# Dense layer with SiLU on one core: where the tail's wait stands, which queue loads the first weight slab, how many dummies, and how the last weight columns are cut

## The chip, the core and the metric

The kernel runs on one core of a Trainium2 chip. The metric is the device time of one execution in microseconds (us). The kernel before took 126.45 us in the median of three runs (126.36 to 126.84). One more execution was profiled; its own time was 126.87 us, and its span, from the first to the last instruction, is 125.4 us.

TensorE (PE) multiplies, ScalarE (ACT) applies the activation, VectorE (DVE) copies results out of PSUM, and SyncE (SP) mostly issues DMAs. ACT can issue DMAs too.

## The reference

```python
# x [1, 2048, 640], w1 [640, 1728], w2 [1728, 640], all bf16
h = einsum("bsd,df->bsf", x, w1)
h = silu(h)
out = einsum("bsf,fd->bsd", h, w2)
```

## The kernel before

**Layout.** The inner width is 1728 = 13 x 128 + 64. Thirteen tiles of 128 rows (`FT`) and a tail of 64 rows (`FL`) make up the hidden layer, kept transposed in `hT` (tokens along the free side) and, for the tail, in `hTt`. The 2048 tokens are cut into four chunks of 512 (`SCH`). The depth 640 of the first product is five tiles of 128 (`DT`).

**The opening.** x must be turned; a transposing DMA writes it to `xT`. A few instructions are moved by `early()` (line 97) ahead of the barrier with which every program begins: the turned load of x for chunk 0, depth tiles 0 and 1 (line 121, on SP); the first half (tiles 0 to 3) of the first weight slab (line 122, on ACT); a memset of `z`; and 20 dummy matmuls on `z` (128x256 each, lines 127 to 135), which keep PE at work until the first data is there. After the barrier SP issues in this order: the second half of the first slab (`ld_w1b`, line 139), slab 1, x tiles 2 and 3, slabs 2 and 3, x tile 4, slab 4, then in one load the columns 1024 to 1727 of all five depth tiles (`ld_rest`, line 146, 880 KB), then 15 turned loads for chunks 1 to 3 of x (line 154), and last w2. ACT, past its barrier, loads its activation table and runs a small activation (line 148).

**First product, chunk 0.** Lines 183 to 193 go depth first: for each of the five depth tiles, PE sweeps the first eight tiles of 128 columns (`NO` = 8) into eight PSUM banks, so that each sweep needs one slab only. Forty matmuls of 128x512 come out of this. Within the first sweep PE waits for `ld_w1b` at tile 4. After the last sweep tiles 8 to 12 follow (lines 203 to 209), five matmuls each, behind one wait for `ld_rest`. ACT turns each finished bank into `hT` (`silu`, line 168).

**First product, the rest.** Chunks 1 to 3 (lines 210 to 217) run tile by tile, each chunk behind a wait for its five turned loads. Then the tail (lines 219 to 227): for each pair of chunks ten matmuls of half the columns, two at a time in two halves of the array, and one ACT activation into `hTt`. `h_last` is the last activation of the full tiles, `h_tail` holds the two of the tail.

**Second product.** `quad()` (line 327) works on four outputs at a time. Each output is a sum over thirteen tiles, which are taken as halves of 64 rows so that two outputs run side by side in the two halves of the array (`lanes`, line 311), plus one matmul on the tail. The order within one half of the work is fixed by `begin()`:

```python
return [lambda ft=ft: u.half(r0, ft, ft == 0, False) for ft in range(FT)] + [end]
```

So thirteen halves come first for each of the two outputs, 26 matmuls in all, and the matmul on the tail (`u.tail()`, in `end`) is the fourteenth. Before the first `quad` stands the wait at line 342 for `h_last` and for both of `h_tail`. The first `quad` does the last 128 of the 640 output columns for all tokens (`Wide`), turned back by DMAs; the others do 512 columns for 128 tokens each (`Tok`). PSUM banks are handed out in turn by `bank()`; each waits for whatever emptied it last. `wait()` (line 69) leaves out a wait for a semaphore value that the same engine has already waited for.

Of the kernel before, what the change touches and what calls it, by code (L numbers as in the profile page):

```python
# [9 lines left out]
def bass_standalone__dense_activation_silu__prompt_kernel(  # L10
# [12 lines left out]
    F = w1.shape[1]  # L23
    P = 128
# [13 lines left out]
    pe, act, dve, pool, sp = nc.tensor, nc.scalar, nc.vector, nc.gpsimd, nc.sync  # L38

    with ExitStack() as es:  # L40
        def sb(name, shape, dtype):
            return es.enter_context(nc.sbuf_tensor(name, shape, dtype))

        xT = sb("xT", [P, DT, S], bf16)
        w1s = sb("w1s", [P, DT, F], bf16)
# [13 lines left out]
        def sem(name):  # L59
            s = es.enter_context(nc.semaphore(name))  # L60
            count[s.name if hasattr(s, "name") else name] = 0
            return [s, 0]

        def tick(ins, s, n=1):
            ins.then_inc(s[0], n)
            s[1] += n
            return (s, s[1])

        def wait(eng, *points):
            for pt in points:  # L70
                if pt is None:
                    continue
                s, v = pt
                key = (id(eng), id(s))
                if seen.get(key, 0) < v:
                    eng.wait_ge(s[0], v)
                    seen[key] = v
# [6 lines left out]
        def load(eng, out_ap, in_ap):  # L84
            s = sem(f"s_ld{n_dma[0]}")
            n_dma[0] += 1
            return tick(eng.dma_start(out=out_ap, in_=in_ap), s, 16)  # L87

        def turned(c0, c1, k0, k1):
            s = sem(f"s_tr{n_dma[0]}")  # L90
            n_dma[0] += 1
            return tick(sp.dma_start_transpose(  # L92
                out=xT[:, k0:k1, c0:c1], in_=xf[c0:c1, k0 * P:k1 * P]), s, 16)

        ET = mybir.EngineType

        def early(emit, engine, arrived=True):
            n = len(nc.main_func.blocks[0].instructions)
            r = emit()
            lst = nc.main_func.blocks[0].instructions  # L100
            new = lst[n:]
            del lst[n:]
            at = next(
                i for i, ins in enumerate(lst)
                if ins.opcode == ("EventSemaphore" if arrived else "Drain") and ins.engine == engine
            )
            lst[at:at] = new
            return r

        w1_v = w1.rearrange("(dt p) f -> p dt f", p=P)  # L110
        w2_v = w2[0:F0, :].rearrange("(ft p) d -> p ft d", p=P)

        NO = NB
        CO = NO * P

        def slab(eng, k, f0=0, f1=NO):
            return load(eng, w1s[:, k, f0 * P:f1 * P], w1_v[:, k, f0 * P:f1 * P])
# [2 lines left out]
        ld_t = {}  # L120
        ld_t[0] = ld_t[1] = early(lambda: turned(0, SCH, 0, 2), ET.SP)
        ld_w1[0] = early(lambda: slab(act, 0, 0, 4), ET.Activation)
        p_z = early(lambda: tick(dve.memset(z[:, :], 0.0), s_dve), ET.DVE, False)  # L123

        bank_free = [None] * NB

        def dummies(n):
            for _ in range(n):
                pe.matmul(ps[:, 3, 0:HB], lhsT=z[:, 0:P], rhs=z[:, :], start=True, stop=True)  # L129

        def first_dummies():
            wait(pe, p_z)
            dummies(20)

        early(first_dummies, ET.PE)

        p_warm = tick(pool.memset(warm[:, :], 0.0), s_pool)  # L137

        ld_w1b = slab(sp, 0, 4, NO)
        ld_w1[1] = slab(sp, 1)  # L140
        ld_t[2] = ld_t[3] = turned(0, SCH, 2, 4)
        ld_w1[2] = slab(sp, 2)
        ld_w1[3] = slab(sp, 3)
        ld_t[4] = turned(0, SCH, 4, 5)
        ld_w1[4] = slab(sp, 4)
        ld_rest = load(sp, w1s[:, :, CO:F], w1_v[:, :, CO:F])
        wait(act, p_warm)
        act.activation(out=warm[:, :], in_=warm[:, :], func=ACT.Silu)  # L148

# [15 lines left out]
        def mm(o, l, r, start, stop, shared=False):  # L165
            return pe.matmul(o, lhsT=l, rhs=r, start=start, stop=stop, skip_group_check=shared)  # L166

        def silu(out_ap, in_ap, bank, after):
            wait(act, after)
            r = tick(act.activation(out=out_ap, in_=in_ap, func=ACT.Silu), s_act)  # L170
            bank_free[bank] = r
            return r
# [24 lines left out]
        def bank():  # L197
            b = nxt[0] % NB
            nxt[0] += 1
            wait(pe, bank_free[b])  # L200
            return b

        wait(pe, ld_rest)
        for ft in range(NO, FT):
            b = bank()
            for k in range(DT):
                ins = mm(ps[:, b, :], w1s[:, k, ft * P:(ft + 1) * P], xT[:, k, 0:SCH],
                         start=(k == 0), stop=(k == DT - 1))
            silu(hT[:, ft, 0:SCH], ps[:, b, :], b, tick(ins, s_pe))
        for c in range(1, NSC):  # L210
            wait(pe, ld_xc[c])
            for ft in range(FT):
# [4 lines left out]
                h_last = silu(hT[:, ft, c * SCH:(c + 1) * SCH], ps[:, b, :], b, tick(ins, s_pe))  # L217
        h_tail = []
# [97 lines left out]

        def begin(u, r0):
            def end():
                u.halfway = tick(u.tail(), s_pe)
            return [lambda ft=ft: u.half(r0, ft, ft == 0, False) for ft in range(FT)] + [end]  # L320

# [5 lines left out]
        def quad(A, B, C, E):  # L327
            A.open()
            B.open()
            lanes(begin(A, 0), begin(B, HP))  # L330
            C.open()
            E.open()
            lanes(begin(C, 0), begin(E, HP))
            for X, Y in ((A, B), (C, E)):
                dx, dy = [], []
                wait(pe, X.halfway, Y.halfway)
                lanes(rest(Y, 0, dy), rest(X, HP, dx))
                X.close(dx[0])
                Y.close(dy[0])

        wait(pe, *ld_w2)
        wait(pe, h_last, *h_tail)
        quad(Wide(0), Wide(1), Wide(2), Wide(3))
        last = None
        for q in range(NSC // 2):
# [56 lines left out]
```

## Time and profile before

| what | value |
|---|---|
| median of three runs | 126.45 us |
| profiled execution, its own time | 126.87 us |
| its span | 125.4 us |
| PE busy | 121.7 us (97%) |
| ACT busy | 38.9 us (31%) |
| DVE busy | 6.9 us (6%) |
| DMA, mean rate over the span | 83 GB/s |

The profile can be asked for groups of instructions, for waits, for the chain of work that ended last, for the work in order of time, for DMAs with their time from issue to landing, and for busy time in chosen stretches. Times in such rows are counted from the start of the span. A matmul's row gives its start and an end that is modelled; matmuls overlap, so the distance between two starts tells the pace. "SPq" and "ACTq" are those engines' issuing of DMAs.

### The profile page before, as it was taken

Reading aid. Unit: us, or ns where it says so; the run is one execution under the profiler, and the core shown is the slowest. Engines: PE = TensorE matmul, PEld = TensorE weight load, DVE = VectorE, ACT = ScalarE, POOL = GpSimd, SP = SyncE. Lnnn points to the kernel's source line nnn. Section 1 sums busy time; section 2 is a strip of 40 time slices with the busy share of each in tenths; the row PEclk is TensorE's granted clock in tenths of the full one; section 3 lists DMA queues with packets and bytes.
Section 4 is the critical chain, followed back from the end, with each engine's and each line's share of the span. In section 5 each row is a group of like instructions: output and inputs, shape, how many; then the busy total and the mean of one; then the engine's idle time right before and its main releaser. Section 6 shows DMA issues by size and latency. Waiting matters only on the chain.

```text
span 125.4 us, 1834 instructions
## 1 busy us (share of the span) xinstructions
PE 121.7 (97%) x822; PEld 60.3 (48%) x828; DVE 6.9 (6%) x11; ACT 38.9 (31%) x67; POOL 0.3 (0%) x5
## 2 busy tenths in 40 slices
PE   8999999999999999999979999999999999999993
PEld 6544344444444444444435555555555555555452
DVE  0000000000000000000000022002200310220201
ACT  4000985555555555555530011001100200110110
POOL 1000000000000000000000000000000000000000
DMA  6999756546990000000000003401300220022032
GB/s 134 234 257 305 163 114 73 100 92 104 363 336 4 0 5 0 3 0 0 0 0 5 0 0 84 89 0 73 136 0 5 105 105 0 5 105 105 0 118 91
DMA packets 18823, 10.38 MB, mean 83 GB/s; under 512 B 13440, under 2 KB 18304, under 8 KB 18816
## 3 DMA queue, kind: packets, MB, share of 16 engines
q1 hardware_dynamic: 18528, 10.08, 31.6%
q10 hardware_dynamic: 288, 0.20, 0.6%
q8 instruction: 6, 0.10, 0.4%
q14 instruction: 1, 0.01, 0.0%
HBM read 4.51 MB, written 2.62 MB: 57 GB/s over the span
## 4 chain that ended last, share of the span: by engine, by line
PE 86%; DMA 6%; SPq 4%; issue 1%; ACT 1%
PE ps L166 86%; DMA w1s<-in_w_dram 6%; SPq L87 2%; SPq L92 2%; ACT hTt L170 0%; ACT o_sb L238 0%
## 5 line engine op out<-in xcount | busy, mean ns | idle before, releaser
L166 PE MATMUL ps<-xT,w1s 128*128 128x512 bf16 (+1 forms) x275 | 58.9, 381 | 0.4 <-DMA w1s<-in_w_dram 0.2
L166 PE MATMUL ps<-w2s,hT 64*128 64x512 bf16 (+3 forms) x402 | 46.3, 370 | 0.2 <-issue 0.2
L166 PEld LDWEIGHTS ps<-xT,w1s 128*128 128x128 bf16 (+1 forms) x280 | 26.5, 99 | 32.6 <-DMA w1s<-in_w_dram 0.7
L170 ACT ACTIVATE hT<-ps 128x512 bf16<-128x512 f32 x52 | 30.1, 605 | 30.0 <-PE ps L166 29.9
L166 PEld LDWEIGHTS ps<-w2s,hT 64*128 64x128 bf16 (+1 forms) x403 | 23.8, 95 | 21.4 <-issue 0.4
L238 ACT CAST o_sb<-ps 128x512 bf16<-128x512 f32 (+1 forms) x9 | 4.9, 550 | 41.6 <-PE ps L166 41.6
L166 PE MATMUL ps<-hT,w2s 64*128 64x512 bf16 x104 | 11.8, 377 | 0.8 <-ACT hTt L170 0.8
L166 PEld LDWEIGHTS ps<-hT,w2s 64*128 64x128 bf16 x104 | 5.8, 94 | 6.4 <-issue 1.2
L236 DVE CAST o_sb<-ps 128x512 bf16<-128x512 f32 (+1 forms) x8 | 5.4, 675 | 40.6 <-PE ps L166 40.6
L236 DVE CAST oT<-ps 128x512 bf16<-128x512 f32 x2 | 1.4, 692 | 75.6 <-PE ps L166 75.6
L129 PE MATMUL ps<-z 128*128 128x256 bf16 x20 | 4.5, 420 | 0.4 <-DVE z L123 0.4
L238 ACT CAST oT<-ps 128x512 bf16<-128x512 f32 x2 | 1.2, 586 | 11.4 <-PE ps L166 11.4
L129 PEld LDWEIGHTS ps<-z 128*128 128x128 bf16 x20 | 2.9, 148 | 1.5 <-DVE z L123 0.4
L166 PE MATMUL ps<-w2t,hTt 64*128 64x512 bf16 (+2 forms) x17 | 3.0, 364 | 0.0
L170 ACT ACTIVATE hTt<-ps 128x512 bf16<-128x512 f32 x2 | 1.2, 597 | 1.1 <-PE ps L166 1.1
L148 ACT ACT_TABLE_LOAD x1 | 1.3, 1283 | 0.7 <-DVEq L387 0.7
L166 PEld LDWEIGHTS ps<-w2t,hTt 64*128 64x128 bf16 x17 | 1.0, 94 | 0.9
L166 PE MATMUL ps<-hTt,w2t 64*128 64x512 bf16 x4 | 0.8, 376 | 0.0
L166 PEld LDWEIGHTS ps<-hTt,w2t 64*128 64x128 bf16 x4 | 0.2, 94 | 0.2
L148 ACT ACTIVATE warm<-warm 128x32 f32<-128x32 f32 x1 | 0.2, 230 | 0.0
L123 DVE MEMSET z<- 128x128 uint32 x1 | 0.2, 165 | 0.2 <-issue 0.2
L137 POOL MEMSET warm<- 128x32 f32 x1 | 0.1, 124 | 0.3 <-POOLq L387 0.3
(4 smaller groups left out, 0.4 us busy)
## 6 DMA issues: line engine op xcount, KB each, us to landing
out_dram<-o_sb SPq DMA_DIRECT2D x15, 160.0 KB, 1.8
w2s<-in_w_dram SPq DMA_DIRECT2D x1, 1120.0 KB, 6.4
w1s<-in_w_dram SPq DMA_DIRECT2D x4, 256.0 KB, 4.1
w2s<-in_w_dram SPq DMA_DIRECT2D x1, 960.0 KB, 8.6
w1s<-in_w_dram SPq DMA_DIRECT2D x1, 880.0 KB, 7.2
xT<-in_x_dram SPq DMA_TRANSPOSE x18, 3.8
w2t<-in_w_dram SPq DMA_DIRECT2D x2, 80.0 KB, 8.0
w1s<-in_w_dram ACTq DMA_DIRECT2D x1, 128.0 KB, 2.4
```

The lines of the kernel that those rows point to most:

```text
L87: return tick(eng.dma_start(out=out_ap, in_=in_ap), s, 16)
L92: return tick(sp.dma_start_transpose(out=xT[:, k0:k1, c0:c1], in_=xf[c0:c1, k0 * P:k1 * P]), s, 16)
L123: p_z = early(lambda: tick(dve.memset(z[:, :], 0.0), s_dve), ET.DVE, False)
L129: pe.matmul(ps[:, 3, 0:HB], lhsT=z[:, 0:P], rhs=z[:, :], start=True, stop=True)
L137: p_warm = tick(pool.memset(warm[:, :], 0.0), s_pool)
L148: act.activation(out=warm[:, :], in_=warm[:, :], func=ACT.Silu)
L166: return pe.matmul(o, lhsT=l, rhs=r, start=start, stop=stop, skip_group_check=shared)
L170: r = tick(act.activation(out=out_ap, in_=in_ap, func=ACT.Silu), s_act)
L236: r = tick(dve.tensor_copy(out=out_ap, in_=in_ap), s_dve)
L238: r = tick(act.copy(out=out_ap, in_=in_ap), s_act)
```

## The change

Four edits. The second half of the first w1 slab is issued by ACT, ahead of the barrier and right behind the first half, and no longer by SP behind it. The dummies go from 20 to 15. The last load of w1 is cut in two, columns 1024 to 1279 (tiles 8 and 9) and columns 1280 to 1727 (tiles 10 to 12 and the tail), and PE waits for the second only at tile 10. The wait for the tail activations leaves the head of the second product; it stands in `end`, right before the matmul that reads `hTt`.

```diff
@@ -120,6 +120,7 @@
         ld_w1[0] = early(lambda: slab(act, 0, 0, 4), ET.Activation)
+        ld_w1b = early(lambda: slab(act, 0, 4, NO), ET.Activation)
         p_z = early(lambda: tick(dve.memset(z[:, :], 0.0), s_dve), ET.DVE, False)
@@ -130,20 +131,21 @@
         def first_dummies():
             wait(pe, p_z)
-            dummies(20)
+            dummies(15)
...
-        ld_w1b = slab(sp, 0, 4, NO)
         ld_w1[1] = slab(sp, 1)
...
-        ld_rest = load(sp, w1s[:, :, CO:F], w1_v[:, :, CO:F])
+        CM = CO + 2 * P
+        ld_rest = load(sp, w1s[:, :, CO:CM], w1_v[:, :, CO:CM])
+        ld_rest2 = load(sp, w1s[:, :, CM:F], w1_v[:, :, CM:F])
@@ -203,6 +205,8 @@
         wait(pe, ld_rest)
         for ft in range(NO, FT):
             b = bank()
+            if ft == NO + 2:
+                wait(pe, ld_rest2)
@@ -316,6 +320,7 @@
             def end():
+                wait(pe, *h_tail)
                 u.halfway = tick(u.tail(), s_pe)
@@ -339,7 +344,7 @@
         wait(pe, *ld_w2)
-        wait(pe, h_last, *h_tail)
+        wait(pe, h_last)
         quad(Wide(0), Wide(1), Wide(2), Wide(3))
```

## The prediction

> **What bounds the kernel now.** I began with the page's busy times: PE is busy for 121.7 of 125.4 us, so anything that shortens the kernel must let PE begin useful work sooner, run it at full pace, or remove a hole. The chain of waits, in order of time, shows the holes:
>
> ```profile
> 6.72 0.04 issue
> 6.77 7.24 DMA w1s<-in_w_dram
> 14.01 0.05 issue
> 14.05 8.59 PE ps L166 x39
> ...
> 64.01 0.02 issue
> 64.03 0.61 ACT hTt L170
> 64.64 0.14 issue
> 64.77 52.96 PE ps L166 x488
> ```
>
> There are two. Up to 14.01 the chain is not PE's but the landing of the 880 KB load (issued at 6.77); at 64.03 PE stands until the second tail activation is done. From 64.77 to 117.7 it is PE alone, so what is gained by then is kept to the end. Next the work of PE in order of time, in the opening and in four very narrow stretches around 4.6, 5.5, 5.7 and 5.9 us, where a row's start is that of the matmul that was running:
>
> ```profile
> 0.39 4.45 PE L129 MATMUL ps<-z 128*128 128x256 bf16 x20 [0.39 <-DVE z L123]
> 4.63 0.63 PE L166 MATMUL ps<-xT,w1s 128*128 128x512 bf16 x1
> 5.06 0.82 PE L166 MATMUL ps<-xT,w1s 128*128 128x512 bf16 x2
> 5.49 0.61 PE L166 MATMUL ps<-xT,w1s 128*128 128x512 bf16 x2
> 5.72 0.59 PE L166 MATMUL ps<-xT,w1s 128*128 128x512 bf16 x2
> ```
>
> The starts tell the pace. Useful matmuls begin at 4.63, are 0.43 us apart up to 5.49, and 0.216 us from then on. The dummies, half as wide, stand (4.63 - 0.39)/20 = 0.212 us apart. So PE runs at half pace for the first 5.1 us of its work, although the granted clock reads 1.00 in every stretch. Third, the DMAs by issue, for the first turned load of x (issued at 0.08), the ACT load and `ld_w1b` (issued at 1.55):
>
> ```profile
> xT<-in_x_dram SPq DMA_TRANSPOSE x1, 3.5
> w1s<-in_w_dram ACTq DMA_DIRECT2D x1, 128.0 KB, 2.4
> w1s<-in_w_dram SPq DMA_DIRECT2D x1, 128.0 KB, 3.1
> ```
>
> What the first useful matmul needs is there at 0.08 + 3.5 = 3.58 us (x) and 0.21 + 2.4 = 2.6 us (weights). PE reaches it at 4.63, because 20 dummies stand ahead of it. Last, the stretches, of which I use the DMA share (second number from the right) and GB/s:
>
> ```profile
> 1.00:2.00 1.00, 1.00 (x7) 0.74 (x5) 0.00 (x0) 1.00 (x1) 0.00 (x0) 1.00 0.63 143
> 2.00:3.00 1.00, 1.00 (x7) 0.69 (x6) 0.00 (x0) 0.25 (x2) 0.00 (x0) 1.00 1.22 259
> 3.00:4.00 1.00, 1.00 (x7) 0.69 (x6) 0.00 (x0) 0.00 (x0) 0.00 (x0) 1.00 0.80 139
> ```
>
> The DMA engines are full from 2 to 3 us, while the turned load is moving, and not before.
>
> **Edit 1: 15 dummies, and `ld_w1b` on ACT.** Five dummies fewer are 5 x 0.212 = 1.06 us: the last one gives way at 3.57, just when x lands now. But `ld_w1b` is issued right behind its first half, at about 0.21 + 0.38 = 0.6 us, so its 131 KB move beside the turned load. At the 259 GB/s of that second they are 0.51 us of DMA time. If they fit into the free share of 1 to 2 us, x lands at 3.58 as now; if all of it is pushed ahead of x, at 4.09. I take 3.9, nearer the full end because most of the turned load moves in the full second. PE starts at most 0.1 later (0.04 from landing to matmul at 14.01, and a weight load of 0.15 in part beside it): 4.0, bounds 3.6 to 4.2. That is 0.63 us earlier, and leaves PE idle from 3.57 to 4.0.
>
> Not all of it counts. If full pace comes at 5.49 again, the half-paced steps cost: before, two steps, 2 x (0.427 - 0.216) = 0.42 us; after, (5.49 - 4.0)/0.427 = 3.5 steps, 0.74. Net gain 0.63 - 0.32 = **0.31 us**. Bounds: full pace by 4.0 gives 0.63 + 0.42 = 1.05; the late clock is a rival below. The Trainium skill, page "TensorE: Matmul & The Clock Gate", Part 1, says that the clock gate opens after a free-running window of about 3.4 us of busy work, whatever the kernel's start. By that rule 5.49 is a draw which another execution would not repeat, the front would be worth anything from nothing to 1.05, and a hole among the dummies could cost a window. The page "DMA: Bandwidth & Descriptors", section "Issuing engines are not separate DMA queues", says that a second queue only saves issue time, as all run on the same 16 engines. It speaks for the late end, 4.2, and a front of 0.21.
>
> Side effects: SP loses one issue of 0.55 us (1.55 to 2.11), so slabs 1 to 4 and x tiles 2 to 4 are issued 0.55 earlier. The tightest now is slab 2: issued at 3.85, 4.3 to landing, 8.15, for PE's seventeenth matmul at 8.52. PE comes 0.31 earlier, the slab up to 0.55: no wait. On ACT the table load and the activation behind it (0.73 to 2.26) slip by 0.38; the first silu is at 12.39. Cost nothing.
>
> **Edit 2: the last columns in two loads.** PE's fortieth matmul starts at 13.49; at 0.216 the next could start at 13.70; it starts at 14.05. The hole is **0.35 us**. The first part is 2/5.5 of the 880 KB, 320 KB. Even if it took as long as the whole does now, 7.24 us from an issue at 6.22, it would land at 13.46; with 320 KB to move I expect it two to three us sooner. PE arrives at 13.70 - 0.31 = 13.39, so the hole closes fully. The second part has ten more matmuls, until 13.39 + 2.16 = 15.55; it is issued about 0.1 earlier than `ld_rest` is now and would have to land 1.5 us later than 14.01 to cost. Rows now are shorter (512 and 896 B against 1408), 640 more of them. At the 342 GB/s of the stretch from 10 to 12 us, 880 KB are 2.6 us; half as much again, 1.3 us, would still fit. SP: one issue more, 0.43 (the issue at 6.77 to 7.2), against the 0.55 saved: the turned loads for chunk 1 are issued at 7.2, as before. Their last is issued at 13.89 and takes 3.9: 17.8. PE needs them at 14.05 + 25 x 0.216 = 19.45 now, 18.8 after. That margin of 1.0 us is what is late next; it is used up if PE gains over 1.6 us by then.
>
> **Edit 3: the tail's wait.** The last pair of tail matmuls starts at 63.61 and the first of the second product at 64.77; at the pace of 0.216 it would be 63.82. The hole is 0.95. With the wait moved, 26 half matmuls stand ahead of it, 13 pairs of 0.216 = 2.8 us, against the activation's end at 64.64: it is over before PE gets there. `h_last` ended at 62.3, w2 and the banks earlier still. What may stay is a change in the array's layout. The nearest row is that from full to half columns, where the starts are 61.33 and 61.64, 0.09 more than a step. I take that: 0.95 - 0.09 = **0.86 us**, bounds 0.77 (PE first runs empty at 64.0) and 0.95. The added wait instructions, 0.05 us each in the sequencer, run ahead of the array: 0 to 0.1 us, I take 0.
>
> **The sum.** 0.31 + 0.35 + 0.86 = 1.52 us off the profiled execution's 126.87: 125.35. That execution is 0.42 above the median. Where the 0.42 lies is not shown; if it is a later landing at 14.01, the edited kernel saves it anyway and 125.35 stands, if it lies elsewhere the median falls to 124.93. I take the middle, 125.1.
>
> **The rivals.** *Only the tail counts.* The half-paced stretch and a late x eat the front, and the part loads land as late as the whole. Then 126.45 - 0.86 = 125.6, or 126.0 from the profiled time. For it: DMA engines full. Against it: 320 KB for 880. *The late clock, slower.* The idle time between 3.57 and 4.0 restarts the 5.1 us that PE took to reach full pace, so this comes at 4.0 + 5.1 = 9.1. Half of 5.1 is lost, 2.55 against 0.42 before: 2.13, less the start's 0.63, 1.5. PE reaches tile 8 at 13.70 + 1.5 = 15.2, 1.15 after the present 14.05; the tail gives 0.86 back: +0.3, 126.75. The kernel is slower if full pace comes after 8.5. For it: the first 1.7 us of dummies did not bring full pace, so busy time is counted strictly. Against it: the hole is small beside the work around it. *The tail's hole stays* because PE waits for something else there: 126.45 - 0.66 = 125.8, or 126.2; every other semaphore it waits for is over by 63.
>
> **The numbers.** My forecast 0.68, only the tail 0.14, the late clock 0.13, the hole that stays 0.05. About 0.5%, 0.63 us, is what a measurement here can tell from no change: faster means below 125.82, slower above 127.08. The forecast lies below but for 0.02; only the tail is split 0.08 to 0.06; the late clock 0.02 faster, 0.07 same, 0.04 slower; the last 0.04 same, 0.01 slower. Together 0.76, 0.19, 0.05. The low end is the best front, 1.05, with 0.35 and 0.86, from the median: 124.2, of which slab 2 takes some, 124.3. The high end takes in only the tail from the profiled time and the hole that stays, 126.2; the late clock is left out.
>
> **What would show it.** PE's first useful matmul at 3.6 to 4.2; starts 0.43 apart until about 5.5; no DMA piece in the chain at 13 to 14; the second product's first matmul 0.2 to 0.4 behind the last tail pair. I am wrong if half pace lasts beyond 7 us, if PE waits for w1 at tile 10 or for x at chunk 1, or if ACT still stands in the chain near 63.

## The result and the profile after

The changed kernel takes 125.44 us in the median of four runs, against 126.63 of four runs of the kernel before: a ratio of 0.990, with a 95% interval from 0.9866 to 0.9934. It is faster, and inside the range. The ratio leaves out executions more than 1.5% above the fastest of their kernel: of the 16 executions of the changed kernel in this study seven, from 126.95 to 127.82 us (127.16 is one of the four above), so that the 1.0% is the gain of the other nine, from 124.85 to 125.51.

The profiled execution took 125.18 us, its span is 123.7: 1.7 us less than before, the same as the difference of the two profiled times. The chain of waits after, in order of time:

```profile
0.09 4.42 DMA xT<-in_x_dram
4.55 7.51 PE ps L168 x34
...
55.28 60.75 PE ps L168 x533
```

Both holes are gone: no landing of w1 at 13 to 14 us, no ACT near 63. What stands at the head instead is the first turned load of x, landing at 4.51 where it landed at 3.55. PE's work in order of time, the dummies as a whole and then what was running around 3.15, 3.3 and 4.8 us:

```profile
0.40 3.11 PE L130 MATMUL ps<-z 128*128 128x256 bf16 x15 [0.40 <-DVE z L124]
...
2.93 0.46 PE L130 MATMUL ps<-z 128*128 128x256 bf16 x2
3.12 0.38 PE L130 MATMUL ps<-z 128*128 128x256 bf16 x2
4.55 0.61 PE L168 MATMUL ps<-xT,w1s 128*128 128x512 bf16 x2 [1.04 <-DMA xT<-in_x_dram]
```

The first useful matmul starts at 4.55, only 0.08 us sooner than before. But the last dummies are already closer than 0.213 us together (2.93, 3.12, and the fifteenth at 3.23), and useful matmuls start at the full pace of 0.22 us at once. The stretch from 3 to 4 us says why PE had to wait:

```profile
3.00:4.00 1.00, 0.51 (x4) 0.19 (x2) 0.00 (x0) 0.00 (x0) 0.00 (x0) 1.00 1.17 275
```

The turned load takes 4.4 us from issue to landing (3.5 before), and the DMA engines are full for one microsecond more (share 1.17, before 0.80). At the seam between the two products:

```profile
62.52 0.60 PE L168 MATMUL ps<-xT,w1s 128*64 128x512 bf16 x4
63.05 0.39 PE L168 MATMUL ps<-hT,w2s 64*128 64x512 bf16 x2
```

The last tail pair starts at 62.74 and the second product at 63.05: 0.31 us, against 1.17 before. So the 1.7 us are 0.85 at the seam and 0.85 up to the first matmul of tile 8 (14.05 before, 13.20 after).

### The profile page after: what moved, and what is told of

Read it like the earlier page. It is cut to its first block, busy times and chain, and to the rows that moved or that the text cites. A ratio compares the mean times of both kernels' runs of the same rounds, so it can differ in the third digit from the quotient of the medians.

```text
span 123.7 us, 1826 instructions
## 1 busy us (share of the span) xinstructions
PE 119.9 (97%) x817; PEld 55.6 (45%) x823; DVE 6.9 (6%) x11; ACT 38.8 (31%) x67; POOL 0.3 (0%) x5
## 3 DMA queue, kind: packets, MB, share of 16 engines
HBM read 4.51 MB, written 2.62 MB: 58 GB/s over the span
## 4 chain that ended last, share of the span: by engine, by line
PE 94%; DMA 4%; issue 0%; ACT 0%; SPq 0%
PE ps L168 94%; DMA xT<-in_x_dram 4%; ACT o_sb L242 0%; SPq L392 0%
## 5 line engine op out<-in xcount | busy, mean ns | idle before, releaser
L168 PE MATMUL ps<-xT,w1s 128*128 128x512 bf16 (+1 forms) x275 | 58.3, 379 | 1.3 <-DMA xT<-in_x_dram 1.0
L168 PEld LDWEIGHTS ps<-w2s,hT 64*128 64x128 bf16 (+1 forms) x403 | 21.1, 94 | 24.2 <-issue 0.4
L168 PEld LDWEIGHTS ps<-hT,w2s 64*128 64x128 bf16 x104 | 5.0, 94 | 6.3 <-issue 0.4
L130 PE MATMUL ps<-z 128*128 128x256 bf16 x15 | 3.1, 395 | 0.4 <-DVE z L124 0.4
L130 PEld LDWEIGHTS ps<-z 128*128 128x128 bf16 x15 | 2.1, 143 | 1.2 <-DVE z L124 0.4
```

## The experiments

My theory after this profile: the tail and the two loads give what the holes showed, the half slab on ACT delays x by as much as the missing dummies would have gained, and the rest of the gain came from full pace being reached at 3.1 us, which another execution need not repeat. The rivals: the opening's edits bring the gain themselves; x is late for another reason; full pace has a fixed place.

**e1, the tail's wait alone**

```diff
             def end():
+                wait(pe, *h_tail)
...
-        wait(pe, h_last, *h_tail)
+        wait(pe, h_last)
```

> The kernel before with only the tail's wait moved. Theory (the hole at the tail is worth what it showed, 0.85 us, and nothing later takes it back): 126.6 - 0.85 = 125.75 us; the first matmul of the second product starts 0.31 us behind the last tail pair; the hole at tile 8 stays, with the 880 KB landing near 14.0. Rival (most of the changed kernel's gain came from the opening): no more than 0.4 us faster, 126.2 or above.

Median 125.67 us against 126.57; ratio 0.9919 (0.9887 to 0.9951). The chain of waits of e1 keeps the hole at tile 8 and has none after it:

```profile
6.75 7.69 DMA w1s<-in_w_dram
14.48 8.59 PE ps L166 x39
...
55.50 61.83 PE ps L166 x538
```

0.81% is 1.0 us (0.6 to 1.4). The theory holds: this edit is most of the change's gain.

**e2, the two loads alone**

```diff
-        ld_rest = load(sp, w1s[:, :, CO:F], w1_v[:, :, CO:F])
+        CM = CO + 2 * P
+        ld_rest = load(sp, w1s[:, :, CO:CM], w1_v[:, :, CO:CM])
+        ld_rest2 = load(sp, w1s[:, :, CM:F], w1_v[:, :, CM:F])
...
+            if ft == NO + 2:
+                wait(pe, ld_rest2)
```

> The kernel before with only the last w1 load cut in two. Theory: the hole of 0.35 us at tile 8 closes and the one at the tail (0.95) stays: 126.6 - 0.35 = 126.25 us, less gain where half pace lasts long. Rival (more and shorter rows make the part land as late as the whole did, or slow the turned loads for chunk 1): PE still waits for w1 at tile 8 or 10 or for x at chunk 1, 126.6 us or above.

Median 126.43 against 126.57; ratio 0.9994 (0.9965 to 1.0022). The hole is gone, and next to nothing is gained. The chain of waits:

```profile
4.85 6.74 PE ps L168 x29
...
63.77 0.61 ACT hTt L172
64.51 52.97 PE ps L168 x488
```

PE never waits for w1 here; in this execution full pace came at 5.7, and PE reached tile 8 at 13.80 by itself. The hole is not equally wide in every execution: in e1's trace, with full pace at 5.2 and the landing at 14.44, it runs from 13.52 (one step behind the fortieth matmul at 13.30) to 14.48, 0.96 us. The gain of this edit is 0.1 us with an interval from -0.3 to 0.4, so the forecast 0.35 is neither confirmed nor excluded.

**e3, the half slab back on SP**

```diff
-        ld_w1b = early(lambda: slab(act, 0, 4, NO), ET.Activation)
...
+        ld_w1b = slab(sp, 0, 4, NO)
         ld_w1[1] = slab(sp, 1)
```

> The changed kernel with the second half of slab 0 back on SP, behind the barrier; 15 dummies, two loads and the moved wait stay. Theory (the second ACT load is what delayed the first turned load of x from 3.58 to 4.51 us): x lands near 3.6 and PE's first useful matmul starts near 3.65, 0.9 us sooner than in the changed kernel; 124.5 us if full pace is reached by then, 125.2 if half pace lasts to 5.5. Rival (x lands late for another reason, such as SP's earlier slab 1): x near 4.4 again, PE at 4.5, 125.4 us or above, since SP has one issue more.

Median 124.97 us (124.57 to 125.69); ratio 0.9901 (0.9866 to 0.9936). x landed at 3.62 and PE started at 3.66, as the theory said. But the edit moves two things at once: the half slab leaves ACT, and on SP slab 1 and the second turned load are issued later again (2.10 and 2.57 in place of 1.55 and 2.10). That it is the ACT load that delays x is therefore argued, from the changed kernel's trace: the half slab's packets there begin from 2.76 to 3.62, among the last of x's, and slab 1's only from 3.37. The rest of the theory missed slab 2. Its wait, in the chain:

```profile
3.85 4.62 DMA w1s<-in_w_dram
8.52 4.06 PE ps L168 x18
```

PE comes to the third sweep at 7.58 and waits until 8.52, so most of the sooner start is lost there. Full pace came at 4.4.

**e4, the changed kernel with 20 dummies**

```diff
-            dummies(15)
+            dummies(20)
```

> The changed kernel with 20 dummies as before. Theory (x lands at 4.4 to 4.5 whatever the dummies do; when full pace comes is a draw): PE starts at 4.6 to 4.7, about 0.1 us later than with 15, without the idle stretch of 1.0 us: 125.5 us. Rival (the number of dummies or the idle stretch decides when full pace comes): full pace again near 5.5 as in the kernel before, 0.4 us more, 125.9 us.

Median 125.56 us, twelve executions from 125.13 to 126.06; ratio 0.9934 (0.9904 to 0.9963). x landed at 4.60, PE started at 4.65 without idling, full pace came at 5.75, as in the rival, yet the median is that of the theory. One trace could not decide this; e5 did.

**e5, the changed kernel again**

> The changed kernel again, as it is, beside the others of this call. Theory (x at about 4.5, PE's start at about 4.55; full pace comes at another time in each execution): 125.4 us; full pace anywhere from 3 to 9 us in the trace, since PE idles for 1.0 us between dummies and data. Rival (full pace comes at a fixed place for this kernel): 3.1 us again.

Twelve executions in two groups with nothing between: six from 124.85 to 125.41, six from 126.95 to 127.82 us. The ratio of 0.992 (0.9881 to 0.9959) is that of the lower group; the median of all twelve is 126.18, against 126.61 of the kernel before beside it. The profiled execution took 127.82. What PE was running around 5.15, 5.55, 9.43, 9.75 and 10.0 us:

```profile
4.77 1.03 PE L168 MATMUL ps<-xT,w1s 128*128 128x512 bf16 x2 [0.99 <-DMA xT<-in_x_dram]
5.17 1.06 PE L168 MATMUL ps<-xT,w1s 128*128 128x512 bf16 x2
9.01 0.95 PE L168 MATMUL ps<-xT,w1s 128*128 128x512 bf16 x2
9.44 0.74 PE L168 MATMUL ps<-xT,w1s 128*128 128x512 bf16 x2
9.79 0.60 PE L168 MATMUL ps<-xT,w1s 128*128 128x512 bf16 x2
```

Starts at 4.77 and 5.17 and at 9.01 and 9.44: PE runs at half pace up to 9.6 us, where the first profile of the same kernel had full pace at 3.1. Half of 4.77 to 9.6 is 2.4 us, about the distance of the groups.

**e6, the half slab on ACT but later**

```diff
-        ld_w1b = early(lambda: slab(act, 0, 4, NO), ET.Activation)
...
         act.activation(out=warm[:, :], in_=warm[:, :], func=ACT.Silu)
+        ld_w1b = slab(act, 0, 4, NO)
```

> The changed kernel with the second half of slab 0 still on ACT, but issued behind the small activation (at about 2.3 us) and not ahead of the barrier. Theory (it delays x only when it moves beside the turned load, and SP's shorter queue is what brings slab 2 in time): x lands near 3.6, PE starts near 3.66, the half slab lands before 5, slab 2 near 7.7, no wait at tile 4 or slab 2 over 0.3 us; 124.7 us with full pace at 4.4, 125.2 with full pace at 5.5. Rival (the half slab lands too late for tile 4, or slab 2 still stands in the way): a wait of 0.5 us or more in the first or third sweep, 125.0 to 125.5 us.

Median 125.27 us (six executions, 125.12 to 125.51); ratio 0.9897 (0.986 to 0.9935). The edit does not do what it was made for. Although it stands behind the activation in ACT's program, the load was issued at 0.90 us, 0.26 later than in the changed kernel (0.64), while ACT was still loading its table and before the activation at 2.03:

```profile
0.73 1.28 ACT L149 ACT_TABLE_LOAD   x1 [0.73 <-PEq L392]
0.90 0.34 ACTq L87 DMA_DIRECT2D w1s<-in_w_dram  x1
```

So it moved beside the turned load again, x landed at 4.46, and the theory was not tested: this is nearly the changed kernel once more. The last of the turned load's 256-byte packets began at 2.88, no later than in the kernel before (3.06), but the load counted as landed 1.58 us after that, against 0.49. Full pace was there at PE's start at 4.51. That all six are near 125.3, though PE idled here too (0.7 us), is not settled by one trace.

**e7, the changed kernel with 6 dummies**

```diff
-            dummies(15)
+            dummies(6)
```

> The changed kernel with 6 dummies in place of 15, so that PE idles from 1.7 to 4.5 us. Theory (full pace needs a mostly busy stretch before it): full pace only between 7 and 10 us, up to 2 us lost to half pace, 126.9 us or so. Rival (idle time among the first 4.5 us does not matter): full pace at 3 to 6 us, 125.4 to 125.8 us.

Median 127.07 us (126.45 to 128.06), slower than before: ratio 1.0053 (1.0023 to 1.0084). The theory holds. PE around 4.85, 6.95, 7.3 and 7.55 us, idle from 1.9 to 4.5:

```profile
4.47 1.03 PE L168 MATMUL ps<-xT,w1s 128*128 128x512 bf16 x2 [2.61 <-DMA xT<-in_x_dram]
6.58 0.93 PE L168 MATMUL ps<-xT,w1s 128*128 128x512 bf16 x2
7.00 0.72 PE L168 MATMUL ps<-xT,w1s 128*128 128x512 bf16 x2
7.35 0.59 PE L168 MATMUL ps<-xT,w1s 128*128 128x512 bf16 x2
```

The first useful matmul is no later than in the changed kernel; full pace comes at 7.3.

**e8 and e11, the kernel before with the tail's wait and the two loads** (the diffs of e1 and e2 together)

> The kernel before with the tail's wait moved and the last w1 load cut in two; the half slab on SP and the 20 dummies stay. Theory (the half slab on ACT and the five dummies bring nearly nothing, because x lands later by what the dummies saved): 125.5 us, the same as the changed kernel within 0.3 us. Rival (the opening's two edits bring what was forecast for them, 0.3 us or more): 125.8 us.

> e8 again (kernel before with the moved wait and the two loads; 20 dummies). Theory (five dummies too many cost 0.3 to 0.6 us where x lands at 3.6): 125.5 us, 0.5 above e3. Rival (what PE gains by starting sooner is lost at slab 2): the same as e3 within 0.2 us.

125.52 us, ratio 0.9902 (0.9868 to 0.9936); again 125.37, ratio 0.9918 (0.9886 to 0.9949), 21 executions from 124.91 to 126.12. That is the changed kernel's lower group within 0.2 us: the opening's two edits together bring nothing that these runs can tell. They may well cost: none of these 21 executions is above 126.12 us, while seven of the changed kernel's 16 are at 126.95 or more. And e4, which has the half slab on ACT besides, is no faster either (0.9934). The trace of e11 shows what is late next: chunk 1 of x landed at 19.40 there, and PE waited 0.4 us for it and 0.4 for slab 2.

**e9, slab 2 on ACT behind x** (the diff is against e3)

```diff
-        ld_w1[2] = slab(sp, 2)
...
         act.activation(out=warm[:, :], in_=warm[:, :], func=ACT.Silu)
+        wait(act, ld_t[0])
+        ld_w1[2] = slab(act, 2)
```

> e3 (half slab on SP, 15 dummies, two loads, moved wait) with slab 2 issued by ACT once the first turned load of x has landed, and no longer by SP. Theory (in e3 slab 2, landing at 8.47, took back 0.94 us of the sooner start): slab 2 lands before 7.6, PE does not wait in the third sweep, and the median is 124.3 us, 0.6 below e3. Rival (whatever moves on a second queue beside a turned load delays that load): x tiles 2 and 3 land after 7.3 instead of 6.6, PE waits in the third sweep all the same, 124.9 us, the same as e3.

Median 125.61 us; ratio 0.9928 (0.9897 to 0.9959). The rival's mechanism fits, and the time is above its 124.9. The turned load of x tiles 2 and 3 took 5.9 us from issue (3.6 in e10, without the ACT load), slab 2 itself landed at 8.74:

```profile
xT<-in_x_dram SPq DMA_TRANSPOSE x1, 5.9
```

```profile
3.40 5.35 DMA w1s<-in_w_dram
8.79 113.79 PE ps L169 x791
```

As in e3, two things move at once: with slab 2 gone, SP issues slab 3 and the third turned load sooner (the latter at 4.47, in e10 at 4.93).

**e10, e3 again**

> e3 again, as it is, beside the others of this call. Theory (no idle stretch among the dummies, so full pace is reached early in every execution): 125.0 us, and no execution above 126.2.

125.04 us (124.84 to 125.59), ratio 0.9879 (0.9838 to 0.992). With e3's, 13 executions of this kernel lie from 124.57 to 125.69. Its medians are the lowest of all kernels tried; the interval overlaps with those of e6, e8 and the changed kernel's lower group. Against e11 on the same chip it gains 0.3 us by its 15 dummies; the intervals overlap.

**e12, e3 with 9 dummies**

```diff
-            dummies(15)
+            dummies(9)
```

> e3 (half slab on SP, two loads, moved wait) with 9 dummies in place of 15, so that PE idles from 2.5 to 3.6 us, for about as long as in the changed kernel, but with nothing on ACT beside the turned load. Theory (an idle stretch of about 1 us before the data puts full pace off in a part of the executions): the times fall into two groups, some near 125 and some 1.5 to 2.5 us above, and full pace comes anywhere from 3 to 9 us. Rival (the load on ACT, not the idle stretch, spoils the changed kernel's opening): all executions between 124.6 and 125.8 us, as in e3.

Median 126.22 us (125.49 to 126.96); ratio 0.9978 (0.9945 to 1.0012): 1.2 us lost against e3. Two groups did not show; the times spread. But the rival (125.8 at most) is out: without any ACT load beside x, an idle stretch is enough. PE in e12 around 3.73, 7.5, 7.85 and 8.07 us:

```profile
3.34 1.03 PE L168 MATMUL ps<-xT,w1s 128*128 128x512 bf16 x2 [0.84 <-DMA xT<-in_x_dram]
7.15 0.87 PE L168 MATMUL ps<-xT,w1s 128*128 128x512 bf16 x2
7.58 0.66 PE L168 MATMUL ps<-xT,w1s 128*128 128x512 bf16 x2
7.86 0.59 PE L168 MATMUL ps<-xT,w1s 128*128 128x512 bf16 x2
```

All traces in one table (us; "idle" is PE's wait for x behind the dummies):

| kernel | dummies | half slab on | x lands | idle | full pace from |
|---|---|---|---|---|---|
| before | 20 | SP | 3.55 | 0 | 5.5 |
| e1, e2 | 20 | SP | 3.56, 3.38 | 0 | 5.2, 5.7 |
| e8, e11 | 20 | SP | 3.42, 3.43 | 0 | 4.1, 3.7 |
| e3, e10 | 15 | SP | 3.62, 3.39 | 0.1 or less | 4.4, 4.6 |
| e9 | 15 | SP (slab 2 on ACT) | 3.37 | 0 | 4.6 |
| e4 | 20 | ACT | 4.60 | 0 | 5.75 |
| changed, e5 | 15 | ACT | 4.51, 4.72 | 1.0 | 3.1, 9.6 |
| e6 | 15 | ACT, 0.26 us later | 4.46 | 0.7 | 4.5 or sooner |
| e7 | 6 | ACT | 4.42 | 2.6 | 7.3 |
| e12 | 9 | SP | 3.29 | 0.8 | 7.7 |

## Why the prediction was right, and where it was not

**The tail's wait: right.** Forecast 0.86, bounds 0.77 to 0.95; the trace shows 0.85, the runs of e1 about 1.0. What stayed is the change of the array's layout, 0.31 - 0.216 = 0.09 us, as taken from the nearest row.

**The two loads: right mechanism, price not confirmed.** Between the profiles of before and after the 0.35 us are all there, and the first part landed at 11.80, well ahead of PE. Alone the edit gains 0.1 us (-0.3 to 0.4). The term was read from one execution as a fixed width, though both edges of the hole move: PE's arrival with full pace, and the landing (14.01 in the kernel before, 14.44 in e1, whose hole is 0.96 us). Why no more of it shows in the median stays open. PE arriving late does not explain it: of the five traces with 20 dummies and the half slab on SP, four reach full pace at 5.5 or sooner.

**The opening: wrong terms.** The forecast had PE start 0.63 us sooner and lose 0.32 to half pace. In the profile it started 0.08 sooner and won 0.42, because full pace came at 3.1; that 0.42 is luck of this execution, as e5 shows, and e8 and e11, without the opening's edits, are as fast as the lower group. The first term was mis-sized at its source: I bounded x's landing at 4.09 by the bytes of the half slab at 259 GB/s, and it is 4.4 to 4.7 in all five traces with that load early on ACT (changed, e4, e5, e6, e7). About 0.5 us is what I had priced by the bytes: the last packet of the turned load begins at 3.56 in place of 3.06. The other 0.45 is time from that packet to the landing, 0.95 in place of 0.49, which no term of mine held. It is 0.48 to 0.50 in all nine traces without that load, and 0.95 to 1.11 in the changed kernel, e4, e5 and e7. The Trainium skill, page "DMA: Bandwidth & Descriptors", section "Issuing engines are not separate DMA queues", says that a second queue saves issue time and no more; e4 beside e8 and e11 agrees (0.9934 against 0.9902 and 0.9918), and e9 shows it can cost more than it saves.

**The late clock: a real case, not a remote one.** I gave it 0.13 and 126.75 us. The changed kernel's upper group is 126.95 to 127.82 us, and the one trace from it shows the rival's sign, full pace not before 9.6, where I had put the limit at 8.5. I had also named half pace beyond 7 us as a sign of being wrong, and this trace has it. The hole it rests on is 1.0 us, where I had 0.43. So the step that failed is again x's landing: the same half microsecond that took the gain from the front made the hole longer. That the idle stretch is the cause rests on e7 and e12, which idle for 2.6 and 0.8 us and are slower as a whole (127.07 and 126.22), and on e4, e8 and e11, which idle for none and have no execution above 126.12. Not explained are e6, which idles for 0.7 us and has no execution above 125.51, and two executions of e9 (126.81 and 127.32), whose trace has no idle stretch ahead of the first useful matmul. Why part of the changed kernel's executions escapes is argued only, below.

**The sum: right in part by luck.** Forecast were 1.35 us off the median of 126.45; measured are 1.0%, 1.27 us. The runs price the terms at about 1.0 (tail), 0.1 (two loads) and nothing that can be told (opening), where I had 0.86, 0.35 and 0.31. So the tail's edit alone is nearly the whole gain, close to the rival "only the tail counts" (125.6), to which I gave 0.14: x was late, as that rival says, while its other condition, part loads as late as the whole, did not come. And PE's first useful matmul at 4.55 lies outside my 3.6 to 4.2.

**What the margins said.** Slab 2 did not hold up the changed kernel (landed 7.66, needed 8.01), as forecast; but in e3, where PE really starts early, it did, so the front's upper bound of 1.05 us, which needs slab 2 by 7.47, was not to be had: with that load on SP it landed at 7.61 to 8.47 in all traces. Chunk 1, named as next, was late once, in e11.

## What to carry to other kernels

Let warm-up dummies reach up to the landing of the first data: five too many cost 0.3 us here, not clear of the noise (e11 beside e10), while too few can cost 2 us of half pace in some executions. Before a load is moved to another queue, look at what it will move beside: here the transposing DMA beside it landed 0.8 us later or more, where the bytes had been priced at 0.5. An edit that places an instruction later in a program need not issue it later (e6): read the issue in the trace. And a hole read from one trace is worth its width only if both its edges stand still from one execution to the next: take several executions' spread as part of the price.

## What the runs showed of the hardware

With a plain load on ACT beside it, the turned load on SP ends late by more than its packets do: from the last packet's start to the landing it took 0.95 to 1.58 us, against 0.48 to 0.50 without; in e9 the two loads beside each other took 5.9 and 5.3 us from issue. In all these runs the loads behind it on SP are issued sooner too, and no run holds those back, so that ACT's load is the cause is likely and not shown.

A DMA that stands behind an activation in ACT's program did not wait for it: in e6 it was issued at 0.90 us, the activation ran at 2.03.

Half pace does not show in the granted clock, which reads 1.00 in every profile here; only the distance of matmul starts tells (0.427 or 0.216 us).

Full pace came as early as 2.7 us after the first dummy (the changed kernel, 3.1) and as late as 9.2 us (e5, 9.6). The Trainium skill, page "TensorE: Matmul & The Clock Gate", Part 1, has a free-running window of 3.41 us that must be busy. As an estimate by that page: windows that ended at full pace were busy for 2.65 of 3.41 us or 78% in the changed kernel; the one before the last in e5 (2.8 to 6.2 us) was busy for 65 to 71% and in e12 (0.9 to 4.3) for 69 to 75%, as the idle time is counted from matmul starts or from the profile's modelled ends, and did not bring it. A limit of about three quarters would fit all traces here, and would let an idle stretch of 1 us matter in some phases and not in others. No run moved the phase on purpose, so this stays an estimate.
